# Phase one of a two-branch kernel: fewer tiles transposed on TensorE, one pair run as single tiles, first norms and one weight matrix moved later

## Chip, cores, metric

One core of a Trainium2 chip. The metric is device microseconds of one execution. A ratio is the mean time of one kernel's fast runs over the mean of the other's of the same rounds, so it is not quite the ratio of the medians that are quoted beside it. The granted clock is the share of TensorE's full speed that the profile says it was given. In the profile's lines PE is TensorE, PEld its weight loads, DVE VectorE, ACT ScalarE, POOL GpSimd, SPq the queue of SyncE.

## The reference, cut to what matters

Two branches, a recurrent memory attention (A) and a shift-and-MLP mixer (B), are added to x. The change touches only the start of branch B, which the kernel calls phase one.

```python
xn = _layernorm(x)                       # "first norm": kept, and written to DRAM for branch A
h  = _gelu(_layernorm(xn) @ w1)          # phase one: "second norm", transpose, matmul, gelu
hs = concat(shifted quarters of h) @ w2  # phase two
x1 = xn + hs                             # then w3, gelu, w4 (phase three), then branch A
out = x + A(xn) + (x1 + h2)
```

x has 2048 rows of 1024 values: 16 tiles of 128 rows. Both norms of a tile come from one set of statistics.

Of the kernel before, what the change touches and what calls it, by code (L numbers as in the profile page):

```python
# [27 lines left out]
NT = S // P  # L28
# [49 lines left out]
def kernel(  # L78
# [48 lines left out]
    def load_consts(n):  # L127
        for _ in range(n):
            t, d = const_loads.pop(0)
            nc.gpsimd.dma_start(t[:], d.ap())  # L130
# [63 lines left out]
    with tc.manual_schedule(engines={mybir.EngineType.PE, mybir.EngineType.SP, mybir.EngineType.Pool}), ExitStack() as actx:  # L194
# [6 lines left out]
        with ExitStack() as bctx:  # L201
# [6 lines left out]
            def load_w3():  # L208

                c, k0 = divmod(w3_at[0], 4)  # L210
                w3_at[0] += 1
                cs = slice(c * (F // 2), (c + 1) * (F // 2))
                nc.sync.dma_start(w3_sb[:, 2 * k0:2 * k0 + 2, cs], w3_v[:, 2 * k0:2 * k0 + 2, cs])

            with ExitStack() as hctx:
# [7 lines left out]
                with ExitStack() as p0:  # L223
                    big = p0.enter_context(tc.tile_pool(name="p0big", bufs=1))
                    ring = p0.enter_context(tc.tile_pool(name="p0ring", bufs=3))
                    w1_sb = big.tile([P, KT, D], BF16)
                    NPE = 6

                    xts = {}

                    def load_x(n):
                        if n < NT:
                            xts[n] = ring.tile([P, D], BF16, tag="xt", bufs=10, name=f"xt{n}")
                            nc.sync.dma_start(xts[n][:], x_v[:, n, :])

                    load_x(0)
                    for c, q in ((0, nc.scalar), (2, nc.scalar), (1, nc.sync), (3, nc.sync)):
                        if q is nc.sync:
                            load_x(1 + c // 2)
                        q.dma_start(w1_sb[:, 2 * c:2 * c + 2, :], w1_v[:, 2 * c:2 * c + 2, :])  # L240
                    for n in range(3, 7):
                        load_x(n)
                    for i in range(4):
                        nc.sync.dma_start(w2_sb[:, 2 * i:2 * i + 2, :], w2_v[:, 2 * i:2 * i + 2, :])
                    for n in range(7, 10):
                        load_x(n)

                    stats = {}

                    def norm_stats(n, part=None):  # L250

                        if n >= NT:
                            return
                        xt = xts[n]
                        if n not in stats:
                            stats[n] = [ring.tile(shape, F32, tag=tag, bufs=6, name=f"{tag}{n}") for tag, shape in (("st", [P, 2, 6]), ("mv", [P, 2]), ("ab", [P, 2]), ("rr", [P, 2]), ("nm2", [P, 1]))]
                        st, mv, ab, rr, nm2 = stats[n]
                        if part in (None, 0):
                            nc.vector.bn_stats(st[:, 0, :], xt[:, 0:512])
                        if part == 0:  # L260
                            return
                        nc.vector.bn_stats(st[:, 1, :], xt[:, 512:1024])  # L262
                        nc.vector.bn_aggr(mv[:], st[:])
                        nc.vector.scalar_tensor_tensor(ab[:], epsm[:], mv[:, 1:2], epsa[:], op0=ALU.mult, op1=ALU.add)
                        nc.gpsimd.tensor_tensor(rr[:], ab[:], neghalf[:], op=ALU.pow)
                        if n >= 8:
                            nc.gpsimd.tensor_scalar(nm2[:], mv[:, 0:1], rr[:, 1:2], -1.0, op0=ALU.mult, op1=ALU.mult)

                    def norm2(n, xn2T, jj):
# [5 lines left out]
                        else:  # L275
                            nc.scalar.activation(xn2[:], xts[n][:], ACTF.Identity, bias=nm2[:], scale=rr[:, 1:2])
                        if n >= NPE:
                            nc.sync.dma_start_transpose(xn2T[:, jj], xn2[:])
                        return xn2

                    def norm1(n):
                        st, mv, ab, rr, nm2 = stats[n]
                        xn = xn_keep[n // 4][:, n % 4]
                        nc.vector.tensor_scalar(xn, xts[n][:], mv[:, 0:1], rr[:, 0:1], op0=ALU.subtract, op1=ALU.mult)
                        nc.gpsimd.dma_start(xn_v[:, n, :], xn)
                        if n < 3:
                            load_x(n + 10)
                        if n in (12, 15):
                            load_w3()
                        return xn  # L290

                    def transposes(xn2, xn2T, jj, half, halves=False):
                        ps = psum0.tile([P, 4, P], F32, tag="tr")
                        for k in range(4):
                            nc.tensor.matmul(ps[:, k, :], xn2[:, (half * 4 + k) * P:(half * 4 + k + 1) * P], ident[:], start=True, stop=True)
                        step = 2 if halves else 4
                        for i in range(0, 4, step):
                            nc.scalar.copy(xn2T[:, jj, half * 4 + i:half * 4 + i + step, :], ps[:, i:i + step])
# [14 lines left out]
                    def stage1(n0, nt, xn2T, between, j0=0):  # L313
                        w = nt * P
                        for co in range(KT):
                            ps = psum.tile([P, 512], F32, tag="mm", bufs=4)
                            for k in range(KT):
                                nc.tensor.matmul(ps[:, :w].rearrange("p (n t) -> p n t", t=P), w1_sb[:, k, co * P:(co + 1) * P],  # L318
                                                 xn2T[:, j0:j0 + nt, k, :], start=(k == 0), stop=(k == KT - 1))
                            nc.scalar.activation(hTB[:, co, 2 + n0 * P:2 + n0 * P + w], ps[:, :w], ACTF.Gelu_apprx_tanh)  # L320
                            for f in between.get(co, ()):
                                f()
# [13 lines left out]
                    tiles2, xn2s = {}, {}  # L336

                    def norm2_of(n):
                        if n % 2 == 0:
                            tiles2[n] = xn2T_tile()  # L340
                        xn2s[n] = norm2(n, tiles2[n - n % 2], n % 2)

                    def tr(n, half, halves=False):
                        transposes(xn2s[n], tiles2[n - n % 2], n % 2, half, halves)
# [6 lines left out]
                    nc.gpsimd.memset(hTB[:, :, 0:2], 0.0)  # L351
                    nc.gpsimd.memset(hTB[:, :, S + 2:S + 4], 0.0)
                    load_consts(4)
                    for n in range(1, 6):
                        if n > 1:
                            norm_stats(n + 1, 0)
                        norm2_of(n)
                        norm_stats(n + 1, 1 if n > 1 else None)
                        if n > 1:
                            norm1(n - 2)  # L360
                        if n == 1:
                            stage1_k(tiles2[0])
                        elif n < 4:
                            stage1(n - 1, 1, tiles2[(n - 1) // 2 * 2], {6 - n: [lambda n=n: tr(n, 0)], 7 - n: [lambda n=n: tr(n, 1)]}, (n - 1) % 2)

                    def ahead(n):
                        norm_stats(n + 1, 0)
                        norm2_of(n)
                        norm_stats(n + 1, 1)
                        norm1(n - 2)  # L370

                    stage1(3, 1, tiles2[2], {0: [lambda: tr(4, 0)], 2: [lambda: tr(4, 1), lambda: ahead(6)], 4: [lambda: tr(5, 0)], 5: [lambda: tr(5, 1), lambda: ahead(7)]}, 1)
                    for n in range(13, NT):
                        load_x(n)

                    def prep(n):
                        norm2_of(n)
                        norm_stats(n + 1)
                        norm1(n - 2)

                    for n0 in range(4, NT, 2):
                        between = {c: [] for c in range(KT)}
                        if n0 + 4 < NT:
                            between[1 + 2 * (n0 == 4)] += [lambda n0=n0: prep(n0 + 4)]
                            between[4 + 2 * (n0 == 4)] += [lambda n0=n0: prep(n0 + 5)]
                        stage1(n0, 2, tiles2[n0], between)
                    for n in (NT - 2, NT - 1):
                        norm1(n)

                xn3T = [wpool.tile([P, 4, KT, P], BF16, tag="w", name=f"xn3T{tb}") for tb in range(4)]  # L390
                with ExitStack() as p2:
# [26 lines left out]
            with ExitStack() as p3:  # L418
# [118 lines left out]
                for tb in range(4):  # L537
# [18 lines left out]
                    for j in range(4):  # L556
                        n = tb * 4 + j
# [216 lines left out]
        ahead = stage_loads([nextB[0]], 0, first_w)  # L774
        for gi_, group in enumerate(groups):
# [3 lines left out]
            for hg in range(8):  # L779
# [8 lines left out]
                if hg < 7:  # L788
                    ahead = stage_loads(Bs, hg + 1, second_w if (gi_, hg) == (0, 0) else ())
                if hg == 7 and gi_ + 1 < len(groups):  # L790
                    ahead = stage_loads([nextB[b] for b in groups[gi_ + 1]], 0)
# [233 lines left out]
```

## The kernel before, where the change touches it

The kernel sets the order of work on VectorE and ScalarE by hand. The matmuls write buffers of PSUM (`ps` in the profile). For each tile: statistics on VectorE (`norm_stats`), the power -1/2 on GpSimd, the second norm (`norm2`, on VectorE for tiles 0 to 7, on ScalarE from 8 on), a transpose (by eight matmuls on TensorE for tiles 0 to 5, by DMA from 6 on), 64 column-group matmuls for one tile or for a pair, a gelu per column group on ScalarE. The first norm (`norm1`) comes two tiles behind.

```python
xts[n] = ring.tile([P, D], BF16, tag="xt", bufs=10)       # x tiles
load_x(0) ... load_x(6); four loads of w2 (2 MB); load_x(7..9)    # all on SyncE's queue
# (cut)
def norm2(n, xn2T, jj):
    xn2 = ring.tile([P, D], BF16, tag="xn2")              # ring of 3 buffers
    if n < 8:   nc.vector.tensor_scalar(xn2, ...)
    else:       nc.scalar.activation(xn2, xts[n], ACTF.Identity, bias=nm2, scale=rr)
    if n >= NPE: nc.sync.dma_start_transpose(xn2T[:, jj], xn2[:])
# (cut)
def stage1(n0, nt, xn2T, between, j0=0):
    for co in range(KT):                                   # 8 column groups
        ps = psum.tile([P, 512], F32, tag="mm", bufs=4)    # 4 PSUM buffers in turn
        for k in range(KT):
            nc.tensor.matmul(ps[...], w1_sb[...], xn2T[:, j0:j0 + nt, k, :], ...)
        nc.scalar.activation(hTB[...], ps[...], ACTF.Gelu_apprx_tanh)
        for f in between.get(co, ()): f()                  # norms of later tiles stand here
```

## Time and profile before

| stretch | us | what bounds it |
|---|---|---|
| phase one | 0 to 66.65 | TensorE |
| phase two | 66.65 to 121.9 | TensorE |
| the rest | 121.9 to 1508.1 | TensorE |

In the 1508.1 us of the profiled span TensorE is busy 99%. The page's busy shares, TensorE's timeline and the timeline of all engines stand in the prediction below.

### The profile page before, as it was taken

To read this page: it belongs to the slowest core of one execution; us is meant where nothing else is said; L and a number is where in the kernel's file an instruction comes from. 1 tells how busy PE (TensorE), PEld (TensorE's weight loads), DVE (VectorE), ACT (ScalarE), POOL (GpSimd) and SP (SyncE) were. 2 spreads that over 40 slices of the span, in tenths; PEclk is the share of its full clock that TensorE was granted. 3 is DMA by queue.
4 is the path that set the end of the run, shared out by engine and by line. 5 is a ranking of instruction groups with operands and counts; after the bars stand their busy time and mean duration, and the time that the engine had idled before them with its cause. 6 is when DMAs were issued, how large, how long until landed. Compare 5 with 4: busy or idle time off the path is not lost.

```text
span 1508.1 us, 24241 instructions
## 1 busy us (share of the span) xinstructions
PE 1498.3 (99%) x9762; PEld 803.5 (53%) x9834; DVE 544.6 (36%) x1136; ACT 501.9 (33%) x1140; POOL 175.6 (12%) x246
## 2 busy tenths in 40 slices
PE   9999999999999999999999999999999999999998
PEld 8744444445444444444456645664665455545555
DVE  8382230100020212221146624651564166516641
ACT  6433103013012011111256614650663266416630
POOL 5241020211111221100000010001000100010001
PEclk9999999999999999999999999999999999999999
DMA  9599762353355787622389956992998299919911
GB/s 313 155 254 329 220 180 88 133 203 113 126 164 147 195 250 253 212 98 84 126 223 254 244 125 175 257 239 68 247 244 203 74 227 228 212 62 200 216 49 51
DMA packets 305380, 272.93 MB, mean 181 GB/s; under 512 B 156023, under 2 KB 272281, under 8 KB 305265
## 3 DMA queue, kind: packets, MB, share of 16 engines
q1 hardware_dynamic: 282800, 189.38, 50.5%
q0 software_dynamic: 21776, 80.85, 15.6%
q8 instruction: 79, 1.29, 0.4%
q10 hardware_dynamic: 688, 1.11, 0.2%
q14 instruction: 37, 0.30, 0.1%
HBM read 190.08 MB, written 45.29 MB: 156 GB/s over the span
## 4 chain that ended last, share of the span: by engine, by line
PE 97%; DVE 1%; DMA 1%; issue 0%; POOL 0%; ACT 0%; SPq 0%; POOLq 0%
PE ps L667 30%; PE pso L725 15%; PE ps L601 15%; PE ps L542 13%; PE ps L568 13%; PE ps L400 4%; PE ps L318 2%; PE psS L682 2%; PE psO L706 2%; PE ps L865 1%; PE ps L492 1%; PE gps L471 0%; PE ps L457 0%; DMA wt<-in_A_Wq_dram 0%; DVE st L262 0%
## 5 line engine op out<-in xcount | busy, mean ns | idle before, releaser
L667 PE MATMUL ps<-hTb,wt 128*128 128x396 bf16 (+2 forms) x2528 | 485.0, 342 | 0.1
L667 PEld LDWEIGHTS <-wt 128*128 128x128 bf16 x2528 | 236.7, 98 | 175.8 <-DMA wt<-in_A_Wq_dram 0.5
L601 PE MATMUL ps<-wt,xT 128*128 128x512 bf16 x1003 | 220.1, 379 | 1.1
L725 PE MATMUL pso<-wo_sb,oX 128*128 128x512 bf16 (+1 forms) x972 | 208.5, 372 | 1.1
L542 PE MATMUL ps<-xn3T,w_sb 128*128 128x512 bf16 x896 | 196.2, 379 | 0.0
L568 PE MATMUL ps<-w_sb,h3T 128*128 128x512 bf16 x873 | 194.3, 379 | 1.2
L601 PEld LDWEIGHTS <-xT 128*128 128x128 bf16 x1024 | 100.2, 98 | 120.8
L543 ACT ACTIVATE h3T<-ps 128x512 bf16<-128x512 f32 x112 | 66.8, 597 | 290.4 <-PE ps L542 289.5
L725 PEld LDWEIGHTS <-oX 128*128 128x128 bf16 x992 | 96.3, 98 | 107.4
L669 ACT CAST KT<-ps 128x462 bf16<-128x462 f32 (+2 forms) x160 | 81.7, 510 | 203.0 <-PE ps L667 198.8
L568 PEld LDWEIGHTS <-h3T 128*128 128x128 bf16 x896 | 87.0, 98 | 103.4
L542 PEld LDWEIGHTS <-w_sb 128*128 128x128 bf16 x896 | 86.6, 98 | 102.0
L688 DVE TENSOR_REDUCE sums<-sm 99x4 f32<-99x396 f32 (+2 forms) x176 | 97.6, 555 | 114.9 <-ACT sm L686 114.9
L671 ACT ACTIVATE QT<-ps 128x462 bf16<-128x462 f32 (+2 forms) x160 | 83.8, 524 | 120.6 <-PE ps L667 106.6
L603 ACT CAST Vs<-ps 128x512 bf16<-128x512 f32 x64 | 37.5, 585 | 233.2 <-PE ps L601 174.9
L684 DVE TENSOR_TENSOR sm<-psS,c_mask_reg_sb 99x396 f32<-99x396 f32 x152 | 86.7, 570 | 71.7 <-PE psS L682 71.4
L607 DVE CAST Vs<-ps 128x512 bf16<-128x512 f32 x64 | 44.3, 692 | 171.6 <-PE ps L601 163.2
L686 ACT ACTIVATE sm<-sm 99x396 f32<-99x396 f32 (+2 forms) x176 | 92.8, 527 | 35.0 <-DVE sm L684 28.2
L694 DVE TENSOR_TENSOR Pn<-sm,rs 99x396 bf16<-99x396 f32 (+2 forms) x176 | 98.9, 562 | 7.1 <-DMA PT<-Pn 0.8
L732 POOL DMA_DIRECT2D out_dram<-ot x30 | 16.4, 546 | 698.9 <-DVE ot L731 693.0
L569 DVE TENSOR_TENSOR R<-ps,R 128x512 f32<-128x512 f32 x32 | 21.9, 689 | 175.3 <-PE ps L568 154.9
L731 DVE TENSOR_TENSOR ot<-pso,Rt 128x512 bf16<-128x512 f32 (+1 forms) x33 | 22.3, 675 | 170.4 <-PE pso L725 166.2
(123 smaller groups left out, 1048.3 us busy)
## 6 DMA issues: line engine op xcount, KB each, us to landing
wt<-in_A_Wq_dram SPq DMA_DIRECT2D x76, 512.0 KB
wt<-in_A_Wk_dram SPq DMA_DIRECT2D x76, 512.0 KB
wt<-in_A_Wv_dram POOLq DMA_DIRECT2D x24, 1024.0 KB, 6.5
V_scratch<-Vs SPq DMA_DIRECT2D x32, 512.0 KB
V<-V_scratch SPq DMA_DIRECT2D x40, 384.0 KB
R_scratch<-x POOLq DMA_DIRECT2D x16, 512.0 KB, 4.7
R<-R_scratch SPq DMA_DIRECT2D x16, 512.0 KB
R_scratch<-R POOLq DMA_DIRECT2D x16, 512.0 KB, 3.8
```

The source lines that it names most:

```text
L542: nc.tensor.matmul(ps[:].rearrange("p (n t) -> p n t", t=P), w3_sb[:, k, f * P:(f + 1) * P], xn3T[tb][:, :, k, :], start=(k == 0), stop=(k ...
L543: nc.scalar.activation(h3T[:, f, :], ps[:], ACTF.Gelu_apprx_tanh)
L568: nc.tensor.matmul(ps[:], h3T[:, f, j * P:(j + 1) * P], w4_sb[:, f, ch * 512:(ch + 1) * 512], start=(f == 0), stop=(f == FT - 1))
L601: nc.tensor.matmul(ps[:], xT[:, m4 * 4 + j, k, :], wv[:, k, :], start=(k == 0), stop=(k == KT - 1))
L667: nc.tensor.matmul(ps[:, :nb], w[:, k, hh * P:(hh + 1) * P], B["hT"][:, k, :nb], start=(k == 0), stop=(k == KT - 1))
L669: nc.scalar.copy(dst[:, hh, :], ps[:, :nb])
L671: nc.scalar.mul(dst[:, hh, :], ps[:, :nb], scale)
L684: nc.vector.tensor_tensor(sm[:T, :, :T], S3, t["mask"][:].unsqueeze(1).to_broadcast((T, 4, T)), op=ALU.add)
L686: nc.scalar.activation(e[:T, :, :T], sm[:T, :, :T], ACTF.Exp, scale=LN2)
L688: nc.vector.tensor_reduce(ss, e[:T, :, :T], axis=AX.X, op=ALU.add)
L694: nc.vector.tensor_tensor(Pn[:T, :, :T], e[:T, :, :T], rs[:T, :].unsqueeze(2).to_broadcast((T, 4, T)), op=ALU.mult)
L725: nc.tensor.matmul(self.ps[:, :self.w], self.oX[0][:, h, self.oX[1] + self.gl * P:self.oX[1] + (self.gl + 1) * P], wo_sb[:, h, self.cc], s ...
```

## The change

The intent, as I read it: take 16 transposes (tiles 4 and 5) off TensorE, bring the second norms of tiles 3 and 4 forward by leaving out first norms before them, keep w2's loads out of the way of x's and of the first transposes, and run tiles 4 and 5 singly so that tile 4 need not wait for tile 5.

```diff
-                    NPE = 6
+                    NPE = 4
-                    for n in range(3, 7):
+                    for n in range(3, 10):
                         load_x(n)
-                    for i in range(4):
+                    def load_w2(i):
                         nc.sync.dma_start(w2_sb[:, 2 * i:2 * i + 2, :], w2_v[:, 2 * i:2 * i + 2, :])
-                    for n in range(7, 10):
-                        load_x(n)
@@ norm1
-                        if n < 3:
-                            load_x(n + 10)
+                        load_x(n + 10)
@@ the tiles (cut: the loop over tiles 1 to 3 without norm1 and without tr(4), tr(5), and the loads of x13 to x15 behind tile 3, which norm1 now issues)
+                    for n in range(4, 8):
                         norm_stats(n + 1, 0)
                         norm2_of(n)
                         norm_stats(n + 1, 1)
-                        norm1(n - 2)
+                        norm1(n - 4)
+                        if n == 5:
+                            load_w2(0)
+                            load_w2(1)
+                            stage1(3, 1, tiles2[2], {}, 1)
+                    load_w2(2)
+                    load_w2(3)
-                    for n0 in range(4, NT, 2):
+                    for n in (4, 5):
+                        stage1(n, 1, tiles2[4], {3: [lambda n=n: prep(n + 4)]}, n % 2)
+                    for n0 in range(6, NT, 2):
                         between = {c: [] for c in range(KT)}
                         if n0 + 4 < NT:
-                            between[1 + 2 * (n0 == 4)] += [lambda n0=n0: prep(n0 + 4)]
-                            between[4 + 2 * (n0 == 4)] += [lambda n0=n0: prep(n0 + 5)]
+                            between[1] += [lambda n0=n0: prep(n0 + 4)]
+                            between[4] += [lambda n0=n0: prep(n0 + 5)]
                         stage1(n0, 2, tiles2[n0], between)
```

`prep(n)` is the second norm of tile n, the statistics of tile n + 1 and a first norm (two of them in prep(10) and prep(11); that edit is cut above). In SyncE's queue the order is now: transpose 4, x10, transpose 5, x11, half of w2, transpose 6, x12, transpose 7, x13, the other half of w2, transpose 8, x14, transpose 9, x15, transposes 10 to 15.

More of the change, by code (lines that the diff above doesn't have):

```diff
@@ L353 @@
                     load_consts(4)
-                    for n in range(1, 6):
+                    for n in range(1, 4):
                         if n > 1:
@@ L358 @@
                         norm_stats(n + 1, 1 if n > 1 else None)
-                        if n > 1:
-                            norm1(n - 2)
                         if n == 1:
                             stage1_k(tiles2[0])
-                        elif n < 4:
+                        else:
                             stage1(n - 1, 1, tiles2[(n - 1) // 2 * 2], {6 - n: [lambda n=n: tr(n, 0)], 7 - n: [lambda n=n: tr(n, 1)]}, (n - 1) % 2)
-                    def ahead(n):
+                    for n in range(4, 8):
                         norm_stats(n + 1, 0)
@@ L369, in ahead @@
                         norm_stats(n + 1, 1)
-                        norm1(n - 2)
-                    stage1(3, 1, tiles2[2], {0: [lambda: tr(4, 0)], 2: [lambda: tr(4, 1), lambda: ahead(6)], 4: [lambda: tr(5, 0)], 5: [lambda: tr(5, 1), lambda: ahead(7)]}, 1)
-                    for n in range(13, NT):
-                        load_x(n)
+                        norm1(n - 4)
[5 more added lines that the diff above has]
+                    load_w2(3)
+                    firsts = list(range(4, NT))
                     def prep(n):
@@ L378, in prep @@
                         norm_stats(n + 1)
-                        norm1(n - 2)
-                    for n0 in range(4, NT, 2):
+                        for _ in range(2 if n in (10, 11) else 1):
+                            norm1(firsts.pop(0))
+                    for n in (4, 5):
+                        stage1(n, 1, tiles2[4], {3: [lambda n=n: prep(n + 4)]}, n % 2)
+                    for n0 in range(6, NT, 2):
                         between = {c: [] for c in range(KT)}
                         if n0 + 4 < NT:
-                            between[1 + 2 * (n0 == 4)] += [lambda n0=n0: prep(n0 + 4)]
-                            between[4 + 2 * (n0 == 4)] += [lambda n0=n0: prep(n0 + 5)]
+                            between[1] += [lambda n0=n0: prep(n0 + 4)]
+                            between[4] += [lambda n0=n0: prep(n0 + 5)]
                         stage1(n0, 2, tiles2[n0], between)
-                    for n in (NT - 2, NT - 1):
-                        norm1(n)
+                    while firsts:
+                        norm1(firsts.pop(0))
                 xn3T = [wpool.tile([P, 4, KT, P], BF16, tag="w", name=f"xn3T{tb}") for tb in range(4)]
```

## The prediction

> **What bounds the kernel now.** I read the page first, its busy shares and its chain of what ended last:
>
> ```profile
> PE 1498.3 (99%) x9762; PEld 803.5 (53%) x9834; DVE 544.6 (36%) x1136; ACT 501.9 (33%) x1140; POOL 175.6 (12%) x246
> ...
> PE 97%; DVE 1%; DMA 1%; issue 0%; POOL 0%; ACT 0%; SPq 0%; POOLq 0%
> ```
>
> TensorE works back to back from start to end, and 97% of the chain is its own stream. So a change pays only what it takes out of, or puts into, that stream: matmuls removed or added, and waits opened. All that this change touches lies in phase one (the first 66.65 us). The view of waits of TensorE for the first 120 us lists two waits only, 1.4 us for the cleared warm-up tile and 0.5 us for the first normalised tile; both are before 8 us, and the change does not touch them. Then the timeline of TensorE alone:
>
> ```profile
> 18.76 1.95 PE L318 MATMUL ps<-xn2T,w_sb 128*128 128x128 bf16 x32
> 20.55 0.39 PE L295 MATMUL ps<-c_ident_sb,xn 128*128 128x128 bf16 x4
> 20.77 1.06 PE L318 MATMUL ps<-xn2T,w_sb 128*128 128x128 bf16 x16
> ...
> 23.68 43.14 PE L318 MATMUL ps<-xn2T,w_sb 128*128 128x128 bf16 x400
> 66.65 3.62 PE L400 MATMUL ps<-w_sb,hTB 128*128 128x512 bf16 x15
> ```
>
> The rows of four are transposes (a half tile each). Four take 20.77 - 20.55 = 0.22 us of the stream, 0.056 each; a 128-column matmul costs the same (16 of them from 20.77 to the next transpose at 21.66: 0.89 us). Of the 32 that start at 18.76, 24 end tile 2, so tile 3 starts at 20.10. With 64 matmuls (3.57 us) and the 16 transposes of tiles 4 and 5 (0.89 us) it ends at 24.56. The six pairs behind it end at 66.65: 7.01 us a pair, 0.1096 us for each 256-column matmul.
>
> Last the timeline of all engines, because the norms move:
>
> ```profile
> 11.98 0.22 DVE L264 SCALAR_TENSOR_TENSOR ab<-epsm,mv,epsa 128x2 f32<-128x2 f32 x1
> 12.29 0.72 POOL L265 TENSOR_TENSOR rr<-ab,neghalf 128x2 f32<-128x2 f32 x1
> 13.04 0.55 DVE L274 TENSOR_SCALAR xn<-xt,mv,rr 128x1024 bf16<-128x1024 bf16 x1 [0.23 <-POOL rr L265]
> ...
> 17.16 0.22 DVE L264 SCALAR_TENSOR_TENSOR ab<-epsm,mv,epsa 128x2 f32<-128x2 f32 x1
> 17.30 0.54 DVE L284 TENSOR_SCALAR xnk<-xt,mv,rr 128x1024 bf16<-128x1024 bf16 x1
> 17.47 0.94 POOL L265 TENSOR_TENSOR rr<-ab,neghalf 128x2 f32<-128x2 f32 x1 [1.07 <-DVE ab L264]
> ...
> 28.02 0.22 DVE L264 SCALAR_TENSOR_TENSOR ab<-epsm,mv,epsa 128x2 f32<-128x2 f32 x1
> 28.26 0.38 ACT L320 ACTIVATE hTB<-ps 128x256 bf16<-128x256 f32 x1 [0.49 <-PE ps L318]
> 28.40 0.87 POOL L265 TENSOR_TENSOR rr<-ab,neghalf 128x2 f32<-128x2 f32 x1 [1.14 <-DVE ab L264]
> 29.37 0.27 POOL L267 TENSOR_SCALAR nm<-mv,rr 128x1 f32<-128x1 f32 x1
> 29.67 1.24 ACT L276 ACTIVATE xn<-xt,nm,rr 128x1024 bf16<-128x1024 bf16 x1 [1.03 <-POOL nm L267]
> 30.82 0.91 ACT L320 ACTIVATE hTB<-ps 128x256 bf16<-128x256 f32 x3
> ```
>
> The last six lines carry my prediction. Tile 8 is the first whose second norm runs on ScalarE. It stands in ScalarE's order behind the fourth gelu of the pair (4, 5); ScalarE waited 1.03 us there for the tile's statistics and worked on it 1.15 us more, so its next gelu began 2.2 us late. TensorE did not feel it: it writes four PSUM buffers in turn, and a pair fills one in 0.88 us, so it had 4 x 0.88 = 3.5 us in hand.
>
> [...]
>
> **The change part by part.**
> 1. Sixteen transposes of tiles 4 and 5 leave TensorE: 16 x 0.056 = -0.89 us. Their four copies (0.58 us each) leave ScalarE, which has slack there.
> 2. Tiles 4 and 5 run singly: 128 x 0.0558 = 7.14 us for 7.01, +0.13.
> 3. First norms four tiles late. Without one, VectorE waits for the power operation at 0.72 us: from "ab" to the next second norm 1.06 us (11.98 to 13.04). Second norm to next "ab" is 1.43 (13.04 to 14.47). So a step takes 2.49 us, for 2.72 with a first norm in it (15.73, 18.44, 21.16, ...). Second norms: tile 2 at 13.04 as before, tile 3 at 15.53, tile 4 at 18.02 (before: 18.44); then with first norms again: tile 5 at 20.73, 6 at 23.44, 7 at 26.16. "ab" of tile 8 then comes at 27.59, only 0.43 us earlier than before.
> 4. w2 behind: the x loads get the queue to themselves, and w2's 2 MB, some 5 us at the 390 GB/s of this stretch, come after about 23 us; needed at 66 us, so free. What matters is tile 4's DMA transpose. Its data is normalised at 18.57. For tile 6 before, the norm ended at 24.43 and the hardware queue's traffic was over at about 27.5 (DMA view by window): 3.1 us; for tile 7, 27.14 to 29.3: 2.2 us. So tile 4 lands between 20.8 and 21.7, ahead of the 23.67 at which TensorE wants it. Tile 5 lands by 24.4, wanted at 27.2; tiles 6 and 7 by about 29, wanted after 30.
> 5. The hidden part. TensorE starts tile 4 at 23.67 instead of 24.56, and a single tile's column group takes 0.446 us instead of 0.88. The norm of tile 8 is still placed behind the fourth group, which now ends at 23.67 + 4 x 0.446 = 25.45 (before 28.07). But its statistics are ready only 1.65 us after "ab" (28.02 to 29.67): at 29.24. ScalarE stands for over 3 us, works 1.15 us, and the gelu of the fifth group ends at 29.24 + 1.15 + 0.28 = 30.67. TensorE has four buffers, now worth 1.78 us: it fills groups five to eight by 27.24, then must wait for that gelu, to about 30.70. Stall: 30.70 - 27.24 = +3.46 us.
> 6. Tile 9's norm, behind group four of tile 5 (about 32.5 us; its statistics are ready at about 31.3): 1.15 + 0.28 us against 1.78 us of buffers, after ScalarE has taken up the group just ended at about 32.85. The gelu behind it ends at 34.3, the buffers at 34.26: +0.1. From tile 6 on the buffers are worth 3.5 us again.
>
> Sum: -0.89 + 0.13 + 3.46 + 0.1 = +2.8 us. Phase two starts at about 69.45 instead of 66.65, and as the rest is a TensorE stream, all of it shows at the end: 1509.73 + 2.8 = 1512.5.
>
> **The rivals.**
> - The plain reading, that the change does what it is for: 1509.73 - 0.76 = 1509.0. For it: TensorE is the bound and loses instructions, and the author moved the norms to bring second norms forward. Against it: VectorE's steps gain 0.43 us while the ScalarE norm moves 2.6 us nearer.
> - The late transpose: TensorE waits at 23.67 for tile 4. For it: issue to landing took up to 3.1 us, and only two samples show it. Against it: 5.1 us are to be had. Even then the stall of step 5 would mostly swallow it, because both end in the same statistics of tile 8: still about 1512.5 unless tile 4 is over 3 us late.
> - [...]
> - VectorE is slowed by something not seen (a buffer held by a transpose in flight: the norm of tile 7 reuses tile 4's buffer, at 26.16, when that should be free). Each us that VectorE loses before tile 8 is a us at the end.
>
> **Range and chances.** The stall has about 0.5 us of doubt on each side from steps 3 and 5. [...] Two per cent are 30 us; nothing here is of that size, so within 2% has all but a little.
>
> **What would show it right or wrong.** Right: in the changed profile TensorE's stream breaks once, near 27.2 us, for some 3.5 us, and the releaser named is ScalarE's gelu into hTB; ScalarE's norm of tile 8 begins near 29.2, behind an idle time of over 3 us that ends with POOL's nm; phase two begins near 69.4. Each step: tile 3 ends at 23.7 (step 1), the second norms of tiles 4, 5 and 6 on VectorE at 18.0, 20.7 and 23.4 (step 3), no wait of TensorE for a transpose (step 4). Wrong: no such break and phase two near 65.9, then I have the order on ScalarE or the buffers wrong; a break at 23.7 that ends with a DMA, then transposes are slower than two samples say; a granted clock under full near 30 us, then the clock rival.

The rival: the clock falls behind the idle time. The range was 1509.2 to 1515.2: its low end is the absence of the stall, its high end was that rival, for which the kernel before, with no such idle time, shows nothing. What the kernel before does show: a matmul took 0.056 us at 128 columns and 0.1096 at 256, so two single tiles cost 0.13 us more than a pair; the gelu at 30.82 began behind the waiting norm of 29.67, though its matmuls, counted, had ended at about 29, which is why step 5 takes ScalarE's work in order; and the power operation took 0.72 us without the first norm beside it and 0.94 with it.

## More of the kernel before

One view I did not weigh there is needed to understand the result: the table by stretches of the kernel before. Its columns are the stretch, its length, the busy time and count of PE, PEld, DVE, ACT and POOL, then PE's granted clock, the DMA engines' mean share and the GB/s they moved.

```profile
14.00:18.00 4.00, 4.00 (x76) 4.00 (x74) 3.86 (x11) 3.04 (x10) 2.16 (x3) 1.00 1.06 370
18.00:22.00 4.00, 4.00 (x75) 4.00 (x73) 3.92 (x9) 3.34 (x11) 2.75 (x4) 1.00 1.06 397
...
26.00:30.00 4.00, 4.00 (x39) 3.58 (x37) 3.89 (x9) 1.50 (x5) 2.55 (x5) 1.00 1.20 171
```

The last two columns say that the DMA engines are full until 22 us with plain loads at 370 to 397 GB/s, w2 among them, and full again from 26 us with DMA transposes, at a share as high and fewer GB/s (26 to 30 us: 1.20 and 171). The share adds up the times of packets, so it can pass 1. From 26 to 38 us there is no hole in which to put 2 MB: in the three stretches of 4 us the share is 1.20, 0.95 and 1.22, and 2 MB are worth 5.4 us of full engines at 390 GB/s.

## The result and the profile after

The changed kernel took 1526.9 us (median of 5 runs, 1525.12 to 1527.18), the kernel before 1510.04 (5 runs, 1509.59 to 1511.12); the ratio is 1.0106 (95% interval 1.0092 to 1.0120). It is slower by 16.9 us, within 2%, but the forecast was 2.8 us more and a range that ended at 1515.2.

Of the changed kernel: the page's busy shares and the chain by engine.

```profile
PE 1500.2 (98%) x9810; PEld 804.6 (53%) x9882; DVE 544.9 (36%) x1136; ACT 501.7 (33%) x1144; POOL 175.1 (11%) x246
...
PE 95%; DMA 3%; DVE 1%; POOL 0%; issue 0%; SPq 0%; ACT 0%; POOLq 0%
```

The chain now holds DMA with 3% where it had 1%. TensorE's waits, longest total first (us in all, times, longest):

```profile
PE ps L316 <- DMA xn2T<-xn: 9.8, 2, 6.4
PE ps L316 <- ACT hTB L318: 2.9, 1, 2.9
PE ps L543 <- DMA w_sb<-in_B_w_dram: 2.0, 2, 1.7
```

The second line is the stall that the prediction was about. The first it had ruled out: two waits for DMA transposes. TensorE's timeline shows where:

```profile
18.64 8.65 PE L316 MATMUL ps<-xn2T,w_sb 128*128 128x128 bf16 x152
30.22 3.73 PE L316 MATMUL ps<-xn2T,w_sb 128*128 128x128 bf16 x64 [2.92 <-ACT hTB L318]
37.34 7.15 PE L316 MATMUL ps<-xn2T,w_sb 128*128 128x256 bf16 x64 [3.40 <-DMA xn2T<-xn]
50.86 30.79 PE L316 MATMUL ps<-xn2T,w_sb 128*128 128x256 bf16 x256 [6.37 <-DMA xn2T<-xn]
81.49 28.87 PE L401 MATMUL ps<-w_sb,hTB 128*128 128x512 bf16 x130
```

Counting with 0.0558 us for each of the 128-column matmuls and 0.1096 for the others: the first stretch ends at 18.64 + 152 x 0.0558 = 27.12, so the gap to 30.22 is 3.10 us. Tile 5 ends at 33.79, pair (6, 7) starts 3.55 us later. It ends at 44.35, pair (8, 9) starts 6.51 us later. The last four pairs take 30.63 us instead of 4 x 7.01 = 28.05: 2.58 us. That last part is the clock, as the stretches say (same columns as above):

```profile
47.00:49.00 2.00, 0.00 (x0) 0.00 (x0) 0.00 (x0) 1.19 (x4) 0.00 (x0) 1.00 1.31 80
49.00:51.00 2.00, 0.14 (x1) 0.14 (x2) 1.50 (x3) 0.00 (x0) 0.00 (x0) 0.64 1.09 315
51.00:53.00 2.00, 2.00 (x11) 1.37 (x10) 1.94 (x5) 0.23 (x1) 1.29 (x3) 0.50 1.02 229
53.00:55.00 2.00, 2.00 (x11) 1.40 (x10) 1.96 (x6) 0.68 (x3) 1.71 (x3) 0.50 0.36 135
```

After these 6.5 us without work, TensorE comes back at a granted clock of 0.50. All in all 3.10 + 3.55 + 6.51 + 2.58 = 15.74, less 0.89 for 16 transposes and 0.12 for an earlier start of this stretch, plus 0.13 for the singles: +14.86 (the transposes and the singles are counted from the cost of one matmul, not measured apart). Phase two starts at 81.49 for 66.65, +14.84. So phase one is accounted for. The profiled execution lost 2.5 us more after it, of which 2.0 are the wait for w3 (third line of the waits).

SyncE's queue shows how the transposes came to be late. The columns are start, length of the issue, and what was issued:

```profile
23.35 0.94 SPq L245 DMA_DIRECT2D w_sb<-in_B_w_dram  x2
24.46 2.01 SPq L277 DMA_TRANSPOSE xn2T<-xn  x1
26.57 0.53 SPq L234 DMA_DIRECT2D xt<-in_A_x_dram  x1
27.20 3.59 SPq L277 DMA_TRANSPOSE xn2T<-xn  x1
...
32.21 1.31 SPq L245 DMA_DIRECT2D w_sb<-in_B_w_dram  x2
33.63 5.85 SPq L277 DMA_TRANSPOSE xn2T<-xn  x1
```

Where w2 is early (the run e1 below) issuing a transpose takes 1.2 to 1.7 us; here it took 2.4 and 1.5 for tiles 4 and 5 and then, with w2 ahead, 2.0, 3.6 and 5.9 us, and what stood behind it on SyncE began only then (the x load behind the 5.9 us at 39.58). In the DMA view by microsecond, packets under 512 bytes are those of transposes (from 19 to 20 us, when only tile 4's was under way, all 500 were such), some 1024 for each. Tile 6's, issued by 26.5, flow only from 30 to 34; tile 8's, issued from 33.6, only from 42 to 46. These are the microseconds from 29, 30, 41 and 42:

```profile
DMA packets 111, 0.21 MB, mean 212 GB/s; under 512 B 8, under 2 KB 8, under 8 KB 111
...
DMA packets 631, 0.31 MB, mean 312 GB/s; under 512 B 575, under 2 KB 575, under 8 KB 629
...
DMA packets 195, 0.39 MB, mean 389 GB/s; under 512 B 17, under 2 KB 17, under 8 KB 195
...
DMA packets 585, 0.24 MB, mean 241 GB/s; under 512 B 532, under 2 KB 532, under 8 KB 585
```

In between flow w2, x and the first norms' stores to DRAM, which GpSimd issues: of the 2.43 MB from 36 to 42 us half (1.22 MB) are on GpSimd's queue.

And the reverse: in the stretch where w2 had been, the DMA engines of the changed kernel have little to move (shares of 0.24 and 0.70).

```profile
14.00:18.00 4.00, 4.00 (x76) 4.00 (x73) 3.49 (x9) 3.03 (x11) 1.38 (x2) 1.00 0.24 71
18.00:22.00 4.00, 4.00 (x76) 4.00 (x74) 3.86 (x11) 3.03 (x11) 1.63 (x2) 1.00 0.70 102
```

71 and 102 GB/s, where the kernel before moved 370 and 397.

### The profile page after: what moved, and what is told of

Its sections match the earlier page's. It is cut to its first block, busy times and chain, and to the rows that moved or that the text cites. A ratio compares the mean times of both kernels' runs of the same rounds, so it can differ in the third digit from the quotient of the medians.

```text
span 1525.4 us, 24347 instructions
## 1 busy us (share of the span) xinstructions
PE 1500.2 (98%) x9810; PEld 804.6 (53%) x9882; DVE 544.9 (36%) x1136; ACT 501.7 (33%) x1144; POOL 175.1 (11%) x246
## 3 DMA queue, kind: packets, MB, share of 16 engines
q10 hardware_dynamic: 688, 1.11, 0.2%
## 4 chain that ended last, share of the span: by engine, by line
PE 95%; DMA 3%; DVE 1%; POOL 0%; issue 0%; SPq 0%; ACT 0%; POOLq 0%
PE ps L668 30%; PE pso L726 14%; PE ps L602 14%; PE ps L569 13%; PE ps L543 12%; PE ps L401 4%; PE ps L316 2%; PE psS L683 2%; PE psO L707 2%; DMA xn2T<-xn 1%; DMA w_sb<-in_B_w_dram 1%; PE ps L866 1%; PE ps L493 1%; PE gps L472 0%; PE ps L458 0%; DMA wt<-in_A_Wq_dram 0%
```

## The experiments

My theory after this (called Q or W in the expectations): w2's 2 MB, put among the DMA transposes, delay those of tiles 6 to 9; TensorE waits for them; the clock drops behind the waits. Beside it stands the ScalarE stall of the prediction's step 5. The rivals: the transposes are slow because x loads are interleaved with them or because there are two more of them; or only the place in SyncE's queue matters, not the traffic.

**e1_w2_early.** The change with w2 back in its old place.

```diff
 for n in range(3, 7): load_x(n)
+for i in range(4): load w2 part i on SyncE
 for n in range(7, 10): load_x(n)
-load_w2(0..3) further down
```

> The changed kernel with the w2 loads back where they were before (early, between the x loads); nothing else. Theory Q (w2's 2 MB, issued between the DMA transposes on the same queue, pushes the transposes of tiles 6 to 9 back): the two waits of TensorE for transposes (3.4 and 6.4 us) and the half clock behind them go, the 2.9 us wait for ScalarE's gelu stays: 1510.0 - 0.9 + 0.1 + 3.0 = about 1512.3. Rival R (the transposes are slow because x loads are interleaved with them or because there are two more of them, w2 or no w2): the waits stay, 1520 or more.

1514.76 us (1512.56 to 1514.96) against 1510.48; ratio 1.0029 (1.0013 to 1.0046). Of TensorE's waits only the one for ScalarE is left in phase one:

```profile
30.92 38.70 PE L317 MATMUL ps<-xn2T,w_sb 128*128 128x128 bf16 x384 [3.55 <-ACT hTB L319]
69.46 55.42 PE L398 MATMUL ps<-w_sb,hTB 128*128 128x512 bf16 x256
```

Phase two starts at 69.46, which is the prediction's 69.45. The profiled execution (1512.56, clock 1.000) is the forecast; the three others took 1514.62 to 1514.96 at mean clocks of 0.997 to 0.999. So w2's new place cost some 12 us, the ScalarE stall the rest, and the stall itself seems to bring the clock down at times (these three were not profiled; in r_after below a clock of 0.50 follows a wait of 2.75 us). x loads and two more transposes, without w2 among them, leave no wait for a transpose here, and 0.7 us of it in e4, where the ScalarE stall no longer hides it: the rival falls as the main cause.

**e2_w2_pool.** The change with `nc.gpsimd.dma_start(w2_sb...)`: w2 at the same time, on GpSimd's queue.

> The changed kernel with its four w2 loads issued from GpSimd's queue at the same places in the program. If the place in SyncE's queue is what hurts (theory Q in its narrow form): waits for transposes nearly gone, 1512 to 1515. If it is the DMA engines' time that w2 takes from the transposes, whatever the queue: still 1520 to 1527. Rival R: no change, about 1526.

1530.19 us (1526.04 to 1531.25); ratio 1.0126 (1.0108 to 1.0144). Worse than the change itself, and above all that I had forecast:

```profile
PE ps L316 <- DMA xn2T<-xn: 14.0, 2, 11.8
```

w2's four loads took 11.0 to 18.6 us to land here, and transpose 7 took 6.56 us to issue though no w2 stood ahead of it on SyncE's queue. So the narrow form, order in one queue, falls. From 18 to 52 us the DMA view counts 61.4% of the 16 DMA engines' time for SyncE's queue and 44.7% for GpSimd's, so the two together filled the same engines; I read from this that it is their time that w2 takes.

**e3_vec_norms.** The change with the second norms of tiles 8 and 9 on VectorE (`n < 8` becomes `n < 10`), so that no norm stands between the gelus of tiles 4 and 5.

> The changed kernel with the second norms of tiles 8 and 9 on VectorE instead of ScalarE, so that no norm stands in ScalarE's order between the gelus of tiles 4 and 5. The 2.9 us wait at 27 us must go. Theory Q: the next wait, for tile 7's transpose at 37.3 us, is set by the queue and not by TensorE, so it grows by what the first one shrank, and the time gains under 1 us: 1524.5 to 1527. If the waits add up independently: about 1523.5.

1519.84 us (1518.82 to 1523.41); ratio 1.0069 (1.0052 to 1.0086). The wait for ScalarE is gone as expected, and the wait at pair (6, 7) grew to 8.4 us: it starts at 39.21, later than in the change. But the wait at pair (8, 9) vanished altogether, so this gained about 7 us where I expected under 1: a miss. Transposes 8 and 9 were issued at nearly the same times as in the change (34.35 and 39.89 us for 33.63 and 40.20), yet had landed by 46.2, when pair (8, 9) starts, and not at 50.9. Why they flowed faster, this run does not say.

**e4_early_vec.** Both edits: w2 early, norms of tiles 8 and 9 on VectorE.

> Both edits: w2 early and the second norms of tiles 8 and 9 on VectorE. Theory Q plus the ScalarE stall of the prediction account for everything: no wait of TensorE in phase one, 16 transposes fewer: 1510.0 - 0.8 = 1509.2 (1508.7 to 1510.2). Rival R: 1518 or more.

1511.39 us (1510.59 to 1512.61); ratio 1.0009 (0.9993 to 1.0026). The two causes together account for all of the loss. The expected gain of 0.8 us did not come: TensorE waited 0.7 us for transpose 7 and 0.5 for a gelu. That is where the 16 transposes saved are given back.

**e5_single.** The kernel before with tiles 4 and 5 run singly and nothing else.

```diff
+for n in (4, 5):
+    stage1(n, 1, tiles2[4], {3: [lambda n=n: prep(n + 4)]}, n % 2)
-for n0 in range(4, NT, 2):
+for n0 in range(6, NT, 2):
```

> The kernel before, with tiles 4 and 5 run singly as in the change and nothing else (transposes of 4 and 5 on TensorE, w2 early, first norms two tiles late). Tests step 5 of the prediction by itself: tile 8's norm on ScalarE now stands behind a group that ends at 24.56 + 1.78 = 26.3 us, its statistics come at 29.7 as before, so TensorE fills its four buffers by 28.1 and waits until about 31.1: +3.0, and +0.1 for the singles: 1513.3 to 1513.8 against 1510.4. If the stall came only from the reordered norms: under 1511.

1514.52 us (1512.33 to 1515.95); ratio 1.0030 (1.0014 to 1.0047). The stall comes from the singles alone:

```profile
30.94 38.70 PE L318 MATMUL ps<-xn2T,w_sb 128*128 128x128 bf16 x384 [2.55 <-ACT hTB L320]
```

The four executions point to the clock's part: 1512.33 at a mean clock of 1.000, 1513.4 and 1515.64 at 0.999, 1515.95 at 0.998. That is 2.1 to 5.7 us over the kernel before; only the first was profiled, so that the wait was the same in all is not shown.

**e6_four_five_pe.** The change with NPE = 6: tiles 4 and 5 on TensorE again, w2 and norms late.

> The changed kernel with tiles 4 and 5 transposed on TensorE after all; w2 late, norms late and singles kept. Theory W (w2's loads and the transposes share the DMA engines badly): the waits for the transposes of tiles 6 to 9 stay for the most part, 1520 to 1527. Rival R2 (it takes the two added DMA transposes to tip it over): waits mostly gone, 1513 to 1515.

1519.25 us (1517.2 to 1521.39); ratio 1.0063 (1.0046 to 1.0080). Half a miss: nothing waits for a transpose on TensorE, but the wait for ScalarE grew from 2.9 to 5.5 us. ScalarE's norm of tile 8 was released at 32.27, when transpose 6 had just landed (its packets end in the microsecond from 31 to 32), not by its statistics, which were ready at 28.9. So transpose 6 is late here too, by way of ScalarE; why this program makes that norm wait for it I did not find out. Two transposes fewer help, but do not cure.

**e7_w2_last_vec.** w2 behind the last transposes of phase one, norms of 8 and 9 on VectorE.

> The changed kernel with w2 loaded behind the last transpose of phase one instead of between them, and the second norms of tiles 8 and 9 on VectorE. Theory W: no wait of TensorE for a transpose, w2's last part lands at about 62 us, ahead of its use at 66: 1509.2 to 1510.8, faster than before by 0.2 to 0.8 us at best. If w2 comes too late: a wait at the start of phase two, 1512 or more. If x loads and transposes alone are enough to delay tiles 6 to 9 (rival R): over 1515.

1511.07 us (1509.99 to 1511.58); ratio 1.0003 (0.9986 to 1.0020). The forecast was no wait for a transpose and at most 1510.8. So late is not bad in itself: issued at 53.9 us, w2 was in time for 67. What hurts is w2 among the transposes between 23 and 46 us (e3, the same kernel with w2 there, took 1519.84). TensorE still waited 1.3 us for transpose 7.

**e8_w2_mid.** The kernel before with w2's four loads between transposes 7 and 8, nothing else.

> The kernel before with w2's four loads moved between the DMA transposes of tiles 7 and 8, nothing else. Pair 8 starts at 38.6 us in the kernel before and its transposes have landed by about 36. If w2 costs the transposes only the time of its own bytes (2 MB at 390 GB/s, 5.2 us): a wait of about 2.5 us, 1512.5 to 1513.5. If mixing loads with transposes slows both (the changed kernel moves 200 GB/s where it mixes them): 1515 to 1525. If neither, 1510.5.

1519.17 us (1518.26 to 1519.76); ratio 1.0056 (1.0039 to 1.0073). One wait:

```profile
46.03 30.50 PE L314 MATMUL ps<-xn2T,w_sb 128*128 128x256 bf16 x256 [7.39 <-DMA xn2T<-xn]
```

This is the change's main cost with no other part of it. The pair starts at 46.0; here the packets of its two transposes were through by about 45.2, before by about 36.6 (counted by quarter of a microsecond). So 2.1 MB, worth 5.4 us of plain loading at 390 GB/s, moved the transposes by some 8.6 us. The granted clock from 42 to 50 us was 0.50. Of my two forecasts (1512.5 to 1513.5 and 1515 to 1525) the second is right.

**e9_first_half_late** and **e10_second_half_late.** The change with only the first or only the second half of w2 late (the other half at the old place).

> The changed kernel with only the first half of w2 (1 MB) behind the transpose of tile 5, the second half early as before. Theory W (what is pushed among the transposes delays the ones behind it): tiles 6 and 7 arrive late as in the changed kernel, so the wait at pair 6 stays near 3 us, and the wait at pair 8 shrinks to under 2 us: 1515 to 1520. If the harm is not in the amount of w2 but in any w2 load there: near 1526.

> The changed kernel with only the second half of w2 (1 MB) late, behind the transpose of tile 7, the first half early. Theory W: pair 6 starts without a wait for DMA after the ScalarE stall, pair 8 waits for tiles 8 and 9, delayed by some 5 us (half of the 10 us that 2 MB cost in the run with w2 mid), against 4 to 5 us in hand: 0 to 2 us of wait, 1513.5 to 1517.

First half: 1518.84 us (1516.82 to 1522.21), ratio 1.0059 (1.0041 to 1.0077), with waits of 2.9 us for ScalarE and 4.1 for a transpose at pair (6, 7), then none at pair (8, 9). Second half: 1514.06 us (1513.65 to 1514.94), ratio 1.0028 (1.0011 to 1.0044), 2.7 us for ScalarE and 0.9 for a transpose, at pair (10, 11). Either half alone costs less than both, and the half that stands ahead of transposes 6 and 7 is the dearer one. The two do not add up: e1 with neither half late lies 4.3 us over its kernel before, the second half 4.1, the first 8.9, both together (r_after, the same rounds) 14.9. So the second half alone costs nothing beyond the stall, and the wait forecast for it at pair (8, 9) did not come.

**e11_early_vec_later.** A try to beat both: w2 behind x tile 9, in the stretch that the change leaves idle, with VectorE norms for tiles 8 and 9, and those of 10 and 11 two column groups later.

> A try for a version that beats both: the changed kernel with w2 loaded early but behind x tile 9 (in the stretch from 14 us on in which the changed kernel leaves the DMA engines idle), the second norms of tiles 8 and 9 on VectorE, and those of tiles 10 and 11 two column groups later. If tiles 6 and 7 land by 30.9 us and ScalarE never waits: 1509.3 to 1510. If tile 7's transpose is still late by about 0.7 to 1.3 us, as in the two runs with VectorE norms before: 1510 to 1511.5, no gain over before.

1510.65 us (1510.06 to 1511.29) against 1509.93; ratio 1.0004 (0.9987 to 1.0020). No gain. TensorE waited 0.7 us for transposes in phase one, and its clock stayed at 1.00.

**r_after.** The change again.

> The changed kernel again, for a second profile. Question: do the 2.5 us that the changed kernel loses after phase one (TensorE waited 2.0 us for the second half of w3) repeat? If they belong to the change: again a wait for w3 of about 2 us and 1525 to 1527. If they were chance of one execution: no such wait, and a profile near 1523 to 1525 with phase one ending near 81 us.

1524.82 us (1522.93 to 1525.85); ratio 1.0101 (1.0084 to 1.0117). No wait for w3 this time, phase one ends at 79.85 and the rest takes 1521.2 - 79.85 = 1441.35 us, as before (1508.1 - 66.65 = 1441.45). So the 2.5 us after phase one were of one execution. And here the clock fell to 0.50 already behind the first, shorter wait (2.75 us, for ScalarE):

```profile
29.00:31.00 2.00, 0.80 (x8) 0.79 (x8) 1.95 (x5) 1.65 (x5) 1.73 (x3) 0.79 1.91 198
31.00:33.00 2.00, 2.00 (x22) 2.00 (x20) 1.93 (x6) 0.59 (x3) 1.80 (x3) 0.50 0.54 168
33.00:35.00 2.00, 2.00 (x34) 2.00 (x32) 1.93 (x6) 1.46 (x3) 1.66 (x4) 0.86 1.20 338
```

The work of tile 5 then took 5.33 us, for 3.73 in the first profile, but pair (6, 7) waited only 1.0 us for its transposes, for 3.4: the two overlap.

One variant was not run: more buffers for x and for the normalised tiles. No run here says what it would do.

## Why the prediction was wrong, point by point

- **Steps 1 and 2, right.** Tile 3 ended at 27.12 - 3.57 = 23.55 (forecast 23.67), a single tile takes 64 x 0.0558 = 3.57.
- **Step 3, right.** Second norms of tiles 4, 5 and 6 at 17.55, 20.24 and 22.96, all about 0.47 us ahead of the forecast, because this execution was 0.4 us ahead already at tile 2; the steps between them are the forecast 2.7.
- **Step 5, right.** TensorE stopped at 27.12 and went on at 30.22: 3.10 us for 3.46; ScalarE's norm of tile 8 began at 28.76 for 29.24, behind 2.94 us of idle time. e5 shows its cause by itself, e1 the sum with it: phase two at 69.46. These are the norms of tiles 8 and 9 on ScalarE:

```profile
28.76 1.24 ACT L275 ACTIVATE xn<-xt,nm,rr 128x1024 bf16<-128x1024 bf16 x1 [2.94 <-POOL nm L266]
...
35.26 1.24 ACT L275 ACTIVATE xn<-xt,nm,rr 128x1024 bf16<-128x1024 bf16 x1 [2.78 <-POOL nm L266]
```

- **Step 4, the step that failed.** It says of w2's loads that they "come after about 23 us; needed at 66 us, so free" and that tiles 6 and 7 land "by about 29, wanted after 30". Tiles 4 and 5 did land in time. Tiles 6 and 7 let TensorE go on at 37.34, tiles 8 and 9 at 50.86. I asked when w2 is needed, and not what it stands in front of: taken as free, it brought waits for transposes of 10.06 us and 2.58 us of low clock behind them. I took the 2.2 to 3.1 us to landing from two transposes that had no w2 ahead of them, and never worked out transposes 8 and 9 at all. The 2.2 us was misread besides: in the kernel before, half of tile 7's 1024 small packets flow from 30 to 31 us, so it landed at 31.0 and not at 29.3, 3.9 us after its norm. e1 (w2 away: the waits go), e8 (w2 alone, put there: the wait comes) and e9 (half of it: a part of the waits) show this part; e10 shows that the second half by itself does little.
- **Step 6, swallowed.** ScalarE's norm of tile 9 began at 35.26, for 32.85. Its buffer is that of tile 6, whose transpose landed late; I read this from the ring of three and the landing, as the profile names the statistics (POOL nm).
- **The rivals.** For the late transpose I said that it would be swallowed by the same statistics; that holds for tile 4 and not for tiles 6 to 9. The clock I gave one chance in six. It fell in every execution of the change (mean clocks of 0.994 to 0.998), costing 2.6 us in the profiled one, there behind the wait for transposes. In e1, without that wait, three of four executions had mean clocks under 1.000 and took 1514.62 to 1514.96. So even with step 4 right the likely time was 1514 to 1515, not 1512.5. VectorE was not slowed: tile 7's second norm began at 25.68, for 26.16. The plain reading, a gain, came true in no run, not even in those without the long waits (e4, e7, e11).

The terms of the sum, forecast and measured: transposes and singles -0.76 and, counted, the same (with 0.12 of an early start apart), ScalarE stall +3.46 and +3.10, tile 9 +0.1 and not apart, waits for transposes 0 and +10.06, clock 0 and +2.58.

What stays open is why 2 MB move the transposes by some 8.6 us and not by 5.4. A part can be counted. From the last packets of transpose 7 to the first of transpose 8 it is 10.65 us in e8 (30.0 to 40.65), for 2.65 before (31.0 to 33.65). In that time SyncE's queue moves 2.73 MB, for 0.68, and GpSimd's 0.93 MB, for 0.26: stores of first norms come in between as well. At 390 GB/s these 0.67 MB more are worth 1.7 us, an estimate; with w2's 5.4 that makes 7.1 of the 8.0 us. Transposes 8 and 9 then take 4.6 us, for 2.9, and why is not known. In some stretches where loads and transposes mix, the engines' share is about full but the rate low (159 GB/s from 30 to 34 us after the change, with a share of 1.19), in others not (352 GB/s from 34 to 38 us, with 1.11). By themselves transposes moved less than the 370 to 397 GB/s of the plain loads: 287 GB/s in e8 from 45 to 46 us, the best of those looked at, and some 1024 packets took from under 1 us (e8: 960 of tile 6's from 26.0 to 26.8 us) to 1.8 us (tile 4 of the change, from 19.4 to 21.2 us). Whether the two kinds hinder each other inside the DMA engines, or the held-up issues on SyncE leave holes, no run here tells apart.

## What to carry to other kernels

A load's price is not when its data are needed but what it is put in front of: before moving one, look at the DMA share by stretch, where it leaves a hole and where it lands. Here 2 MB cost a wait of 7.4 us ahead of two transposes (e8), and behind the last one they were still in time (e7). When a stage is cut into smaller pieces, its fixed number of buffers covers less time (here 1.78 us for 3.5), so any norm or copy placed between the pieces needs its inputs earlier (e5: a wait of 2.55 us from this alone). A wait of TensorE of some 3 us brought a spell at a clock of 0.50 on top in some executions and not in others: it did after 2.75 us in r_after, and did not after 2.92 us in the first profile of the change, nor after 2.55 and 3.55 us in the profiled executions of e5 and e1 (mean clocks of 1.000).
